# Fused attention and two MLPs on one core: the last pair of a long attention block is multiplied by v behind the next block's first tile, and v is loaded a head earlier

## The chip, the cores and the metric

One core of a Trainium2 chip runs the whole program in one launch. The metric is the device time of the execution in microseconds; lower is better. A run before the change takes 764.3 us (median of three).

## The reference

Causal attention with a decay (4 batches, 8 heads, 576 rows, head width 64), then a residual MLP behind a layer norm, then a gated MLP with a product over the sequence:

```python
scores = scale * np.matmul(q, k.transpose(0, 1, 3, 2))
decay = cum[:, :, :, None] - cum[:, :, None, :]
scores = np.where(causal, -1000000000.0, scores + decay)
...
attn = attn / (np.sum(attn, axis=-1, keepdims=True) + 1e-09)
return np.matmul(attn, v).astype(np.float32)
...
ch = np.maximum(xn @ w_ch1, 0.0) @ w_ch2
return (x + ch).astype(np.float32)
...
v_s = np.einsum('ts,bsd->btd', w_spatial, v_n) + b_spatial[None, :, None]
gated = u * v_s
return (gated @ w_out).astype(np.float32)
```

Here `cum` is the running sum of log f along the rows, `xn` the layer norm of x, `u` and `v_n` the two halves of relu(x @ w_in), the second one normed.

## The kernel before

Attention is cut into eight blocks of 256 rows of x (`BLOCKS`), and the first MLP into seven groups that follow them one group behind. Blocks 0 to 3 hold the first 128 and the second 128 rows of two batches each. Blocks 4 to 7 are the four long ones, one for each batch: query rows 256 to 575 against all keys up to them (`attention`, line 571). They run from about 200 to 460 us, between the matmuls of the first MLP (lines 849 and 864), of which each group has 384.

A long block goes over four pairs of heads. For each head, `operands` (line 325) loads q and k (qk) and four rows of decay into one of three buffers x2z, and splits q and k in two parts for an exact product. `weights` (line 345) then makes one tile of 128 query rows: scores on TensorE (line 359), mask and minimum on VectorE (363), exponential and sum on ScalarE (367), reciprocal (370), a high half on ScalarE (319) and a low half on VectorE (380, called `low`), and a transposing DMA of both halves from SyncE into PT (382). Tiles 2 and 3 belong to one head; tile 4, the last 64 rows, is made for both heads of the pair at once and has two cuts of 288 columns. When a pair's three tiles are transposed for both heads, `values` (line 578) multiplies them by v: 30 small matmuls into one bank (line 586), evicted by ScalarE (591, 592). v's columns for the pair are loaded as vr (610) and split in two halves vp by ScalarE and VectorE (`parts16`, 280 and 281). The product of a pair is called in the next pair, behind its second head's tile 3; the product of the last pair is called two steps after its tile 4 (lines 623 and 624).

The order of the work is written in two stages. `run` gives each block's and each MLP group's steps a time on a common line (`SPAN`, `BEGIN`, `steps`, line 1368) and calls them in that order; the next block begins before the one before it has ended. That order is a priority. The scheduler of the framework then places every instruction on its engine's queue by what it reckons to be ready, so a change of one priority shifts many places on every queue. Each engine, and SyncE's DMA queue, executes in its order. `after` adds an order between two instructions, here "not placed before".

Of the kernel before, what the change touches and what calls it, by code (L numbers as in the profile page):

```python
# [23 lines left out]
NP = H // 2  # L24
# [1 line left out]
TOK = 256  # L26
QW = S - 2 * P
SC = 2.0 ** 14
BUFS = dict(vr=1, vp=2, qk=3, x1=3, x2=3, PT=4, sd=3, st=6, P16=5, xt=1)
BUFS0 = dict(vr=1, qk=1, e=4, diag=2, PT=2, st=4)  # L30
BUFS1B = dict(vr=4, vp=4, qk=4, sd=4, P16=4, PT=3, st=8)
BUFS1 = dict(vr=3, vp=3, qk=3, sd=2, P16=2, PT=2, st=6)
# [9 lines left out]
BLOCKS = [(0, 0), (2, 0), (0, 1), (2, 1), (0, 2), (1, 2), (2, 2), (3, 2)]  # L42
# [6 lines left out]
RAMP, G1 = 1.5, 1.0  # L49
BEGIN = [0.0, G1, *(RAMP + 0.5 * i for i in range(6)), RAMP + 3.5]  # L50
E0, E1 = -0.1, 0.45
SPAN = [(-1.0, -0.6), (0.02, 0.45), (0.46, RAMP - 0.47), (RAMP - 0.46, RAMP - 0.14)]
for _n in range(4):
    SPAN.append((SPAN[-1][1] - (0.065 if _n else 0), SPAN[-1][1] + 2.39 / 4))
SPAN.append((SPAN[-1][1] - 0.034, SPAN[-1][1] + 0.02))
RAWAT = (-0.975, -0.974, -0.973)
CONV = (-0.6, 0.001, 0.002, 0.003, 0.004)
# [18 lines left out]
def qtile(i):  # L76
    return i * P, min(S, (i + 1) * P)
# [11 lines left out]
class Kernel:  # L89
# [235 lines left out]
    def operands(self, bh):  # L325

        nc, at = self.nc, self.at
        W, C = QW, QW + S
        qk = at.tile([P, C], F32, tag="qk", name="qk", bufs=BUFS["qk"])
        nc.sync.dma_start(out=qk, in_=self.qk[bh // H, bh % H])  # L330
        x1 = at.tile([P, C], F32R, tag="x1", name="x1", bufs=BUFS["x1"])
        if not self.x2z:
            for i in range(BUFS["x2"]):
                self.x2z.append(at.tile([P, C], F32R, name=f"x2z{i}"))
# [10 lines left out]
    def weights(self, i, heads):  # L345

        nc, at, bufs, q0 = self.nc, self.at, BUFS, 2 * P
        lo, hi = qtile(i)
        R, N, nb, qs, m0 = hi - lo, hi, i + 1, slice(lo - q0, hi - q0), 512 - lo
        M = R * len(heads)  # L350
        sd = at.tile([P, S], F32, tag="sd", name="sd", bufs=bufs["sd"])
        st = at.tile([P, 5], F32, tag="st", name="st", bufs=bufs["st"])
        cuts = [(0, N)] if N <= 512 else [(0, 288), (288, 576)]
        for n, (c0, c1) in enumerate(cuts):
            ps = self.bank("s")
            for u in reversed(range(len(heads))):

                for g, (x, y) in enumerate(heads[u][0]):
                    nc.tensor.matmul(  # L359
                        ps[: R * u + R, : c1 - c0], lhsT=x[:, lo - q0 - R * u : hi - q0], rhs=y[:, c0:c1],  # L360
                        start=g == 0, stop=g == len(heads[u][0]) - 1, skip_group_check=True)
            mask = self.mask4[:M] if n else self.mask[:M, m0 + c0 : m0 + c1]
            nc.vector.tensor_tensor_reduce(  # L363
                out=sd[:M, c0:c1], in0=ps[:M, : c1 - c0], in1=mask, scale=-0.125,
                scalar=3e38 if n == 0 else st[:M, n - 1 : n], op0=ALU.add, op1=ALU.min, accum_out=st[:M, n : n + 1])
        n = len(cuts) - 1
        nc.scalar.activation(sd[:M, :N], sd[:M, :N], AF.Exp, bias=st[:M, n : n + 1], scale=-1.0, accum_out=st[:M, 2:3])  # L367
        rs = st[:M, 3:4]
        nc.scalar.activation(rs, st[:M, 2:3], AF.Copy, bias=1e-9 / SC, scale=1.0 / SC)
        nc.vector.reciprocal(rs, rs)  # L370
        ph = at.tile([P, 5, 2, P], F16, tag="P16", name="P16", bufs=bufs["P16"])
        pieces = [(0, i), (i, nb)] if R < P else [(0, nb)]
        if R < P:
            nc.gpsimd.memset(ph[:M, i, :, R:], 0.0)
        for k0, k1 in pieces:
            w = P if k1 * P <= N else R
            src = sd[:M, k0 * P : k0 * P + (k1 - k0 - 1) * P + w].rearrange("p (t w) -> p t w", w=w)
            dh, dl = ph[:M, k0:k1, 0, :w], ph[:M, k0:k1, 1, :w]
            self.copy(DHE[i - 2], dh, src, rs)
            low = nc.vector.scalar_tensor_tensor(out=dl, in0=src, scalar=rs, in1=dh, op0=ALU.mult, op1=ALU.subtract)  # L380
        for u, (_, PT) in enumerate(heads):
            tr = nc.sync.dma_start_transpose(out=PT[:, : 2 * nb, qs], in_=ph[R * u : R * u + R, :nb].rearrange("p t h w -> p (t h w)"))
            self.in_order("tr", tr)
        return low


# [184 lines left out]
    def attention(self, b, xT, xt, middle=None):  # L571
        nc, at, bufs = self.nc, self.at, BUFS
        q0, W = 2 * P, QW
        stored = xt is None
        if stored:
            xt = at.tile([P, NP, S - 512], F32, tag="xt", name="xt", bufs=bufs["xt"])

        def values(p, vp, vsc, heads, behind=None):

            pav = self.bank("av")  # L580
            for kt in range(5):
                n0 = max(kt * P, q0) - q0
                for vi, pi in ((0, 1), (1, 0), (0, 0)):
                    for u in range(2):
                        us = slice(64 * u, 64 * u + 64)
                        ins = nc.tensor.matmul(  # L586
                            pav[us, n0:W], lhsT=vp[:, vi, kt, us], rhs=heads[u][1][:, 2 * kt + pi, n0:W],
                            start=(kt == 0 and (vi, pi) == (0, 1)), stop=(kt == 4 and (vi, pi) == (0, 0)), skip_group_check=True)
                        if behind is not None and kt == 0 and (vi, pi) == (0, 1):
                            self.after(ins, behind)  # L590
            nc.scalar.activation(xT[:, p, :], pav[:, :TOK], AF.Copy, scale=vsc)
            nc.scalar.activation(xt[:, p, :], pav[:, TOK:W], AF.Copy, scale=vsc)
            if p == 1:
                self.xs = self.mo_sum(xT)
            elif p == 2:
                nc.vector.tensor_tensor(out=self.xs, in0=self.xs, in1=xT[:, 2, :], op=ALU.add)

        late = None
        passes = self.operands(b * H)
        for p in range(NP):  # L600
            if middle and p == 2:
                middle()
            heads = []
            for u in range(2):
                heads.append((passes, at.tile([P, 10, W], F16, tag="PT", name="PT", bufs=bufs["PT"])))
                if 2 * p + u + 1 < H:
                    passes = self.operands(b * H + 2 * p + u + 1)
                if u:
                    vr = at.tile([P, 5, P], F32, tag="vr", name="vr", bufs=bufs["vr"])
                    nc.sync.dma_start(out=vr, in_=self.v[b, :, p * P : (p + 1) * P].rearrange("(t p) d -> p t d", p=P))  # L610
                yield
                for i in (2, 3):
                    done = self.weights(i, heads[u:])
                    if late and (u, i) == (1, 3):
                        yield
                        values(*late, done)
                    yield
            vp = at.tile([P, 2, 5, P], F16, tag="vp", name="vp", bufs=bufs["vp"])
            self.weights(4, heads)
            vsc = self.parts16(vr, vp[:, 0], vp[:, 1], b)  # L620
            late = p, vp, vsc, heads
            yield
        yield
        values(*late)
        yield
        if stored:
            nc.scalar.dma_start(out=self.xt_d[:, :, b, :], in_=xt)
        return self.xs
# [658 lines left out]
    def run(self):  # L1287
# [77 lines left out]
                yield  # L1365


        steps = [(NP * 2 + 1, NP * 6, NP * 8 + 1)[kind] + 3 for _, kind in BLOCKS] + [4]
        events = []
        for n in range(last + 1):  # L1370
            a0, a1 = SPAN[n]
            events += [(a0 + (a1 - a0) * (e + 0.5) / steps[n], 1, n) for e in range(steps[n])]
# [90 lines left out]
        for b in range(B):  # L1463
            x2 = self.load_x2(b + 1) if b + 1 < B else iter(())
# [69 lines left out]
```

## Time and profile before

| | |
|---|---|
| median of 3 runs | 764.3 us (762.98 to 765.41) |
| profiled execution | 763.16 us, of which the span of its instructions 761.2 us |
| TensorE busy | 739.7 us, 97%, clock 1.0 |
| VectorE, ScalarE busy | 590.9 us (78%), 528.8 us (69%) |
| long blocks, 200 to 460 us | TensorE 253.49, VectorE 218.41, ScalarE 209.00 us busy |

The page of a profile has the busy time of each engine, the span in 40 slices, the chain of work that ended last and the costliest groups of instructions. Beside it the trace answers questions: a timeline of one engine in a stretch, where the bracket behind a row tells how long the engine was idle before it and what ended that; a table of waits by what ended them; busy time by stretches; the chain in a stretch, in which a DMA's row runs from its issue to its landing.

### The profile page before, as it was taken

What the parts mean: (1) busy time and instruction counts of PE and PEld (TensorE: products, weight loads), DVE (VectorE), ACT (ScalarE), POOL (GpSimd) and SP (SyncE); (2) the same over time, 40 slices, a digit from 0 to 9 for tenths busy, and PEclk for the clock granted to TensorE, in tenths of its full rate; (3) what the DMA queues carried; (4) which work ended last, traced back from release to release, by engine and by line L of the source; (5) the groups of instructions that cost most, each with busy time, mean ns of one, the idle gap of its engine ahead of it and who ended that gap; (6) DMA issues with size and microseconds to landing.
All of it is one profiled execution on the core that took longest, in us unless ns stands there. A gap on an engine that the chain in (4) does not pass through costs nothing.

```text
span 761.2 us, 16265 instructions
## 1 busy us (share of the span) xinstructions
PE 739.7 (97%) x5912; PEld 567.9 (75%) x5912; DVE 590.9 (78%) x1569; ACT 528.8 (69%) x1320; POOL 67.4 (9%) x102
## 2 busy tenths in 40 slices
PE   8899998999999999999999999999999999999998
PEld 6788887888888877877888888644447678768686
DVE  7899799577599989989869845689456796785854
ACT  6898699576588989879857844587346764664633
POOL 6001100013102010110110100200012000000000
PEclk9999999999999999999999999999999999999999
DMA  8978694466589998988965944831025240100101
GB/s 263 295 269 274 206 266 84 89 171 105 176 167 206 198 220 183 195 189 177 201 144 116 148 84 149 213 132 56 1 22 111 70 125 1 44 21 7 57 2 62
DMA packets 164100, 104.68 MB, mean 138 GB/s; under 512 B 106147, under 2 KB 151299, under 8 KB 164021
## 3 DMA queue, kind: packets, MB, share of 16 engines
q1 hardware_dynamic: 153032, 93.06, 50.3%
q0 software_dynamic: 5376, 5.54, 5.2%
q10 hardware_dynamic: 5612, 5.06, 2.2%
q8 instruction: 46, 0.75, 0.4%
q14 instruction: 34, 0.27, 0.1%
HBM read 64.37 MB, written 15.11 MB: 104 GB/s over the span
## 4 chain that ended last, share of the span: by engine, by line
PE 63%; DVE 11%; ACT 10%; DMA 10%; issue 4%; SPq 2%; DVEq 0%; ACTq 0%
PE ph L864 16%; PE acc L849 12%; PE pb L808 8%; PE pb L809 8%; PE pb L810 8%; DMA raw<-in_moe_w_ch_dram 3%; PE s L359 3%; PE s L849 3%; DMA vr<-in_v_dram 2%; PE av L586 2%; ACT wt L744 2%; ACT P L319 2%; DMA x_d<-xT 2%; DVE P L380 1%; DMA qk<-decay 1%
## 5 line engine op out<-in xcount | busy, mean ns | idle before, releaser
L849 PE MATMUL acc<-hh,wt 128*128 128x256 f16 (+2 forms) x960 | 196.8, 295 | 3.2 <-ACT hh L875 3.2
L864 PE MATMUL ph<-xh,wt 128*128 128x256 f16 (+1 forms) x896 | 185.0, 288 | 2.0 <-DVE hl L879 2.0
L864 PEld LDWEIGHTS <-wt 128*128 128x128 f16 x1344 | 126.9, 98 | 47.4 <-issue 10.2
L849 PEld LDWEIGHTS <-wt 128*128 128x128 f16 x1344 | 128.7, 98 | 44.3 <-issue 5.3
L864 PE MATMUL ph<-xl,wt 128*128 128x256 f16 (+1 forms) x448 | 129.0, 288 | 0.0
L849 PE MATMUL acc<-hl,wt 128*128 128x256 f16 (+1 forms) x416 | 115.8, 281 | 1.1 <-DVE hl L879 1.1
L875 ACT ACTIVATE hh<-ph 128x256 f16<-128x256 f32 (+2 forms) x128 | 50.9, 397 | 45.8 <-PE ph L864 45.5
L879 DVE SCALAR_TENSOR_TENSOR hl<-ph,hh 128x256 f16<-128x256 f32 (+1 forms) x112 | 50.5, 453 | 35.9 <-ACT hh L875 35.7
L319 ACT ACTIVATE P<-sd,st 128x512 f16<-128x512 f32 (+2 forms) x128 | 70.6, 585 | 9.8 <-DVE st L370 6.9
L380 DVE SCALAR_TENSOR_TENSOR P<-sd,st,P 128x384 f16<-128x384 f32 (+2 forms) x96 | 59.2, 634 | 10.5 <-ACT P L319 10.3
L367 ACT ACTIVATE sd<-sd,st 128x384 f32<-128x384 f32 (+2 forms) x80 | 54.6, 682 | 14.4 <-DVE st L363 14.2
L359 PE MATMUL s<-x2z 128*128 128x384 f32 (+3 forms) x128 | 47.8, 382 | 1.9 <-DMA x2z<-decay_d 1.7
L363 DVE CUSTOM_DVE_ANT_0 sd<-s,mask 128x384 f32<-128x384 f32 (+2 forms) x80 | 46.0, 579 | 3.7 <-PE s L359 2.7
L900 POOL DMA_DIRECT2D x_d<-t x36 | 31.9, 1024 | 182.7 <-DVE t L896 153.1
L359 PE MATMUL s<-x 128*128 128x384 f32 (+3 forms) x128 | 41.4, 333 | 0.0
L809 PE MATMUL pb<-wsl,vh 128*128 128x288 f16 x128 | 36.6, 286 | 0.0
L808 PE MATMUL pb<-wsh,vl 128*128 128x288 f16 x128 | 36.6, 286 | 0.0
L810 PE MATMUL pb<-wsh,vh 128*128 128x288 f16 x128 | 36.4, 286 | 0.0
L810 PE MATMUL pb<-gh,woh 128*128 128x288 f16 x128 | 35.0, 286 | 0.0
L809 PE MATMUL pb<-gl,woh 128*128 128x288 f16 x128 | 35.0, 286 | 0.0
L808 PE MATMUL pb<-gh,wol 128*128 128x288 f16 x128 | 33.3, 286 | 0.0
L922 ACT ACTIVATE gh<-u 128x288 f16<-128x288 f32 x32 | 14.0, 437 | 26.5 <-DVE u L1261 26.5
(341 smaller groups left out, 1692.5 us busy)
## 6 DMA issues: line engine op xcount, KB each, us to landing
raw<-in_moe_w_ch_dram SPq DMA_DIRECT2D x32, 512.0 KB
qk<-in_qk_dram SPq DMA_DIRECT2D x32, 448.0 KB
vraw<-in_v_dram SPq DMA_DIRECT2D x5, 1024.0 KB
vr<-in_v_dram SPq DMA_DIRECT2D x16, 320.0 KB
x_d<-t POOLq DMA_DIRECT2D x36, 128.0 KB, 4.3
out_dram<-o SPq DMA_DIRECT2D x32, 144.0 KB
raw<-in_moe_w_in_dram SPq DMA_DIRECT2D x8, 512.0 KB
qk<-in_qk_dram SPq DMA_DIRECT2D x16, 192.0 KB
```

The source lines that it names most:

```text
L319: self.nc.scalar.activation(out, in_, AF.Copy, scale=scale)
L359: nc.tensor.matmul(ps[: R * u + R, : c1 - c0], lhsT=x[:, lo - q0 - R * u : hi - q0], rhs=y[:, c0:c1], start=g == 0, stop=g == len(heads[u] ...
L363: nc.vector.tensor_tensor_reduce(out=sd[:M, c0:c1], in0=ps[:M, : c1 - c0], in1=mask, scale=-0.125, scalar=3e38 if n == 0 else st[:M, n - 1 ...
L367: nc.scalar.activation(sd[:M, :N], sd[:M, :N], AF.Exp, bias=st[:M, n : n + 1], scale=-1.0, accum_out=st[:M, 2:3])
L380: low = nc.vector.scalar_tensor_tensor(out=dl, in0=src, scalar=rs, in1=dh, op0=ALU.mult, op1=ALU.subtract)
L808: first = mm(out, lhsT=al, rhs=bh, start=start, stop=False, **kw)
L809: mm(out, lhsT=ah, rhs=bl, start=False, stop=False, **kw)
L810: mm(out, lhsT=ah, rhs=bh, start=False, stop=stop, **kw)
L849: ins = nc.tensor.matmul(acc[m], lhsT=a, rhs=b, start=bank not in clear, stop=last and e == len(terms) - 1, skip_group_check=True)
L864: ins = nc.tensor.matmul(ph, lhsT=a, rhs=b, start=k == e == 0, stop=k == NK - 1 and e == len(terms) - 1)
L875: relu = nc.scalar.activation(hh, ph, AF.Relu)
L879: nc.vector.scalar_tensor_tensor(out=hl, in0=ph, scalar=0.0, in1=hh, op0=ALU.max, op1=ALU.subtract)
```

## The change

Three edits, with their consequences in the tables of steps. The buffer of vr gets a second copy, and v is loaded with a pair's first head instead of its second. The product of a block's last pair is called three steps after its tile 4 and two more (`LATER`) steps of the block exist, so that it is called when the next block has begun. And its first matmuls are placed behind `self.low`, the low half of the tile that was made last by then: one of the next block's first tiles, or in the last block its own tile 4.

```diff
-BUFS = dict(vr=1, vp=2, qk=3, x1=3, x2=3, PT=4, sd=3, st=6, P16=5, xt=1)
+BUFS = dict(vr=2, vp=2, qk=3, x1=3, x2=3, PT=4, sd=3, st=6, P16=5, xt=1)
...
+LATER = 2
 SPAN = [(-1.0, -0.6), (0.02, 0.45), (0.46, RAMP - 0.47), (RAMP - 0.46, RAMP - 0.14)]
 for _n in range(4):
-    SPAN.append((SPAN[-1][1] - (0.065 if _n else 0), SPAN[-1][1] + 2.39 / 4))
+    _a = SPAN[3][1] + 2.39 / 4 * _n - 0.065 * (_n > 0)
+    _b = SPAN[3][1] + 2.39 / 4 * (_n + 1)
+    SPAN.append((_a, _b + (_b - _a) / 28 * LATER))
...
+        self.low = low
         return low
...
-                if u:
+                if not u:
                     vr = at.tile([P, 5, P], F32, tag="vr", name="vr", bufs=bufs["vr"])
                     nc.sync.dma_start(out=vr, in_=self.v[b, :, p * P : (p + 1) * P].rearrange("(t p) d -> p t d", p=P))
...
-        yield
-        values(*late)
+        for _ in range(1 + LATER):
+            yield
+        values(*late, self.low)
...
-        steps = [(NP * 2 + 1, NP * 6, NP * 8 + 1)[kind] + 3 for _, kind in BLOCKS] + [4]
+        steps = [(NP * 2 + 1, NP * 6, NP * 8 + 1 + LATER)[kind] + 3 for _, kind in BLOCKS] + [4]
```

In the changed file line 359 stands at 362, 382 at 385, 610 at 614, 338 at 341, 586 at 590, and 849 and 864 at 854 and 869.

**TensorE, end of the first long block.** From the last scores of its last pair (bank s2_3324) to the product by v (av). Of the matmuls in between, those of the MLP (ph, acc) and of other tiles' scores are left out. Before:

```order
L359 MATMUL s2_3324<-x2z0_2347 64x288
L359 MATMUL s2_3324<-x1_2917 64x288
...
L864 MATMUL ph_4076<-xl_3606,wt_171 128x256
L586 LDWEIGHTS vp_3315
L586 MATMUL av_3372<-PT_3101,vp_3315 64x320
L864 LDWEIGHTS wt_171
L864 MATMUL ph_4076<-xh_3605,wt_171 128x256
L359 MATMUL s2_3692<-x2z1_2349 128x384
L359 MATMUL s2_3692<-x1_3534 128x384
...
L586 MATMUL av_3372<-PT_3194,vp_3315 64x320
```

And now:

```order
L362 MATMUL s2_3324<-x2z0_2347 64x288
L362 MATMUL s2_3324<-x1_2919 64x288
...
L362 MATMUL s2_3694<-x2z1_2349 128x384
L362 MATMUL s2_3694<-x1_3513 128x384
...
L869 MATMUL ph_4153<-xh_3603,wt_171 128x256
L590 LDWEIGHTS vp_3315
L590 MATMUL av_3448<-PT_3101,vp_3315 64x320
L590 LDWEIGHTS vp_3315
L590 MATMUL av_3448<-PT_3196,vp_3315 64x320
```

The first matmul of the product stood alone, ahead of a tile of the next block's second pair, with the other 29 behind; now all 30 stand together behind that tile. Between the last scores and the first of the 30 there were 64 matmuls of the MLP and are 99.

**TensorE, last pair of the last long block.** From the last scores of the pair before (s2_6509, the last reader of x2z1) to the last head's first scores (s2_6643, which read x2z1 as newly loaded). Before:

```order
L359 MATMUL s2_6509<-x2z1_2349 64x288
L359 MATMUL s2_6509<-x1_6053 64x288
...
L359 MATMUL s2_6556<-x2z0_2347 128x384
L359 MATMUL s2_6556<-x1_6334 128x384
...
L359 MATMUL s2_6643<-x2z1_2349 128x384
```

And now:

```order
L362 MATMUL s2_6509<-x2z1_2349 64x288
L362 MATMUL s2_6509<-x1_6055 64x288
...
L362 MATMUL s2_6558<-x2z0_2347 128x384
L362 MATMUL s2_6558<-x1_6336 128x384
...
L362 MATMUL s2_6643<-x2z1_2349 128x384
```

The rows are the same, but in between there were 36 matmuls of the MLP and the 30 of a product by v, and now there are 14 matmuls of the MLP and no product.

**SyncE, the same place.** The queue's transposing DMAs (PT), loads of v (vr) and of decay rows (x2z). Before:

```order
L382 DMA_TRANSPOSE PT_6238<-P16_6298 128x8x128
L610 DMA vr_6610<-in_v_dram 128x5x128
L382 DMA_TRANSPOSE PT_6331<-P16_6380 128x6x128
L338 DMA x2z1_2349<-decay_d_68 4x896
L382 DMA_TRANSPOSE PT_6331<-P16_6393 128x8x128
```

And now:

```order
L385 DMA_TRANSPOSE PT_6238<-P16_6329 128x8x128
L385 DMA_TRANSPOSE PT_6333<-P16_6380 128x6x128
L385 DMA_TRANSPOSE PT_6333<-P16_6393 128x8x128
L341 DMA x2z1_2349<-decay_d_68 4x896
L385 DMA_TRANSPOSE PT_6238<-P16_6518 128x10x64
```

The load of v has left this place (it went out with the pair's first head), and the load of x2z1 stands behind both of the second head's first two transpositions instead of one.

## Rows read from the trace of the kernel before

**Rows 1.** The page, part 1: busy us, share of the span and instructions.

```profile
PE 739.7 (97%) x5912; PEld 567.9 (75%) x5912; DVE 590.9 (78%) x1569; ACT 528.8 (69%) x1320; POOL 67.4 (9%) x102
```

**Rows 2.** Busy time by stretches: length, then each engine, granted clock, DMA.

```profile
200.00:460.00 260.00, 253.49 (x2342) 210.30 (x2340) 218.41 (x593) 209.00 (x542) 26.04 (x40) 1.00 0.85 167
```

**Rows 3.** TensorE's waits from 190 to 470 us: total, times, longest.

```profile
PE av L586 <- DMA PT<-P: 2.7, 2, 1.7
PE s L359 <- DMA x2z<-decay_d: 1.7, 2, 1.5
PE acc L849 <- DVE hl L879: 1.1, 1, 1.1
```

**Rows 4.** The chain from 425 to 435.5 us: start, us, what.

```profile
427.48 1.06 PE s L359 x8
...
429.32 1.68 PE av L586 x30
...
431.66 0.81 PE s L359 x4
...
433.79 1.31 PE acc L849 x12
```

**Rows 5.** TensorE's timeline (start, us, instruction), end of the first long block.

```profile
254.77 0.29 PE L359 MATMUL s<-x 128*64 128x288 f32 x1
...
266.45 0.27 PE L864 MATMUL ph<-xl,wt 128*128 128x256 f16 x1
268.40 0.30 PE L586 MATMUL av<-PT,vp 128*64 128x320 f16 x1 [1.68 <-DMA PT<-P]
```

**Rows 6.** The same, end of the second long block.

```profile
310.05 0.28 PE L849 MATMUL acc<-hl,wt 128*128 128x256 f16 x1
...
324.55 0.30 PE L586 MATMUL av<-PT,vp 128*64 128x320 f16 x1 [1.04 <-DMA PT<-P]
```

**Rows 7.** The same, third long block, third pair.

```profile
339.70 0.28 PE L849 MATMUL acc<-hh,wt 128*128 128x256 f16 x1
...
348.41 0.41 PE L359 MATMUL s<-x2z 128*128 128x384 f32 x1 [1.49 <-DMA x2z<-decay_d]
```

**Rows 8.** The same, fourth long block, first pair's second head.

```profile
378.76 0.41 PE L359 MATMUL s<-x2z 128*128 128x384 f32 x1 [0.26 <-DMA x2z<-decay_d]
```

**Rows 9.** Fourth long block, last pair: timelines of three engines, and the chain's end.

```profile
428.39 0.28 PE L864 MATMUL ph<-xh,wt 128*128 128x256 f16 x1
...
428.38 2.66 POOL L900 DMA_DIRECT2D x_d<-t  x3 [2.27 <-DVE t L896]
...
430.33 0.70 SPq L338 DMA_DIRECT2D x2z<-decay_d  x1
...
435.10 0.12 issue
435.22 0.41 PE s L359
```

**Rows 10.** The chain behind v's load, first long block; then TensorE's timeline.

```profile
208.88 3.36 DMA vr<-in_v_dram
...
218.93 0.27 PE L864 MATMUL ph<-xh,wt 128*128 128x256 f16 x1 [0.71 <-DVE hl L879]
```

**Rows 11.** TensorE's timeline, end of the third long block.

```profile
372.23 0.39 PE L849 MATMUL acc<-hh,wt 128*128 128x256 f16 x2
...
385.21 0.32 PE L586 MATMUL av<-PT,vp 128*64 128x320 f16 x1
...
386.56 0.73 PE L586 MATMUL av<-PT,vp 128*64 128x320 f16 x8
```

**Rows 12.** The chain over the whole span: two loads of x2z, issue to landing.

```profile
346.27 2.01 DMA x2z<-decay_d
...
373.04 5.58 DMA x2z<-decay_d
```

**Rows 13.** Busy time by stretches, as in the second group.

```profile
340.00:360.00 20.00, 18.51 (x169) 15.52 (x169) 19.49 (x53) 18.64 (x50) 0.66 (x3) 1.00 0.83 166
```

## Prediction, made before the changed kernel was run

> **What bounds the kernel now.** The page's first part says TensorE is busy for 739.7 of 761.2 us, 97% [rows 1]: only time in which TensorE stands still can be won. The table of stretches says where that is in the part that the change touches: from 200 to 460 us, while attention and the first MLP share the engines, TensorE is busy 253.49 of 260 us at a granted clock of 1.00, and VectorE 218.41 and ScalarE 209.00 [rows 2]. So there are 6.5 us to win there and no more. The table of waits names what ended TensorE's idle time [rows 3]: the transposed weights PT (a DMA) before the product by v, 2.7 us in two waits; the decay rows loaded into x2z before a tile's scores, 1.7 us; hl from VectorE, 1.1 us, beside a shorter one.
>
> The timeline then gives the place of each. An MLP matmul is shown 0.27 us wide, but the next one starts 0.11 us later (12 take 1.31 us [rows 4]), so a wait costs 0.16 us more than the idle time printed: at 268.40 the loss is 268.40 - 266.45 - 0.11 = 1.84 us where 1.68 is printed [rows 5]. With that the waits cost: product by v at the end of the first long block 1.84 and of the second 1.20 [rows 5, 6]; scores behind x2z 1.65, 0.42 and 0.28 [rows 7, 8, 9]; hl 0.87 and 1.27 [rows 3, 10].
>
> **How much cover each of them has.** Between the end of a pair's last scores and its product by v, TensorE does other work; the transposed weights need a fixed chain in that time (mask, exponential, sum, two halves, transposing DMA). In the first long block the last scores end at 254.77 + 0.14 = 254.9 and the weights are there at 268.40: the chain needs 13.5 us [rows 5]. In the second it is 324.55 - 310.05 = 14.5 [rows 6]. In the third no wait is shown: at most 385.21 - 372.23 = 13.0 for the first head's weights and 386.56 - 372.23 = 14.3 for the second's [rows 11].
>
> The order before puts 64, 79 and 86 MLP matmuls between the two in these blocks, plus other blocks' scores and one earlier product by v. At 0.109 us a matmul, 1.68 for a product by v, 0.81 for a head's first two tiles and 1.06 for a tile of both heads [rows 4] that is 11.5, 13.2 and 12.4 us of cover. The order of the changed kernel has 99, 111 and 96 matmuls, and one more pass of scores in the first two: 15.8, 17.1 and 13.3 us. In the fourth block it has 77 both before and after: there the operand named as "behind" is the block's own last tile, so nothing moves.
>
> **The change part by part.**
> The move of the last product: 15.8 us of cover against 13.5 needed, and 17.1 against 14.5. Both waits go: -1.84 - 1.20 = -3.04 us. What they give back isn't lost to a later stage: xT of a long block is used by the MLP group that begins some 270 MLP matmuls later (about 30 us), so the norm, its SyncE and ScalarE stores and the split of x can all come 4 us later at no cost; that cover would have to shrink by tens of us to matter. In the third block the product now is in one piece of 30, so it needs both heads' weights, between 13.0 and 14.3 us after the scores, and has 13.3. A wait of 0 to 1.0 us; I take 0.4, a little under the middle, as nothing shows that the second head's weights came only just before they were read.
>
> v's load: it moves from the pair's second head to its first, into the other buffer. 16 loads before and after, and as many conversions; nothing is added. What goes is that SyncE's queue must hold the load until VectorE has converted the pair before. That shows at the start of the first long block: v's load leaves at 208.88, right behind that conversion, and lands 3.36 us later, ScalarE goes on with it at once, and the chain ends in the hl for which TensorE waits at 218.93 [rows 10]. In the new order both conversions stand early, but the same exponentials and both heads' conversions of q and k still stand ahead of that hl. Of 0.87 us between all and nothing is won; I take half, -0.4.
>
> What the two parts shift in SyncE's and TensorE's orders: each second head's x2z has to wait for the last scores of the pair before (the buffer is shared), then passes SyncE's queue and lands. In the third block's third pair this needs 348.41 - 339.70 = 8.7 us [rows 7]; TensorE's order had 6.8 us of work in that time and now has 79 matmuls and two tiles, 9.8 us: -1.65. At the fourth block's first pair it needs 6.5 us [rows 11, 8] and now has over 13: -0.42. At the last pair of the last block it is the other way: the order before has 36 matmuls, a product by v and two tiles, 6.5 us, and the need is 435.22 - 428.39 = 6.8 [rows 9]; the new order has 14 matmuls and two tiles, 1.53 + 0.81 = 2.3 us. Here the price of the load decides. It lands 2.01 us after its issue where the queue is quiet, 5.58 where other transfers are under way, and at this place 435.10 - 430.33 = 4.8 [rows 12, 9]; before it, SyncE spent 1.9 us after the release on v's load and a transposition, which now stand earlier. With 0.4 us to issue, the need lies between 2.4 and 6.8 us, so the new wait between 0 and 4.5. The nearest row is this load's own, since the accumulating stores of the MLP group that ends here, three of them from 428.38 on [rows 9], stay at this place: 0.4 + 4.8 = 5.2, a wait of 2.9, which with the 0.28 of before is +2.6.
>
> The Trainium skill has a rule for this price: the page "DMA: Bandwidth & Descriptors", section "Anatomy of one DMA", gives a fixed cost of about 2.0 us and a part that grows with the size (told there of GpSimd's queue). By it the 14 KB would land in 2.0 us and the new wait would be nothing, the sum -5.4; the 2.01 us row agrees, the 4.8 and 5.58 rows do not.
>
> The second hl wait (1.27) and what the scheduler reshuffles on VectorE and ScalarE I leave at nothing: same instructions, same counts, other order.
>
> Sum: -3.04 + 0.4 - 0.4 - 1.65 - 0.42 + 2.6 = -2.5 us. The profiled execution took 763.16 us, so 760.7 against it; that execution lies 1.1 under the median of 764.3, and against the median the forecast is **761.8 us**. A measurement of this kernel can tell about 0.3%, 2.3 us, from no change: faster is below 762.0, slower above 766.6.
>
> **The rivals.**
> Quiet load: the last x2z lands in 2 us, as at 346.27 [rows 12]. No new wait: -2.5 - 2.9 = -5.4, 758.9 us. For it: v's load, which stood directly before it, is gone from there. Against it: the stores at the group's end stay. This is also what the page's rule above gives. Chance 0.22.
>
> The waits only change their place: the last x2z needs the full 6.8 us although v's load is gone (wait 4.5 instead of 2.9), the third block's product pays its full 1.0, and the early hl gives back nothing. -2.5 + 1.6 + 0.6 + 0.4 = +0.1: 764.4 us, no change. For it: two of three x2z waits on record landed late [rows 9, 12]. Chance 0.20.
>
> Slower, by VectorE: the chain from scores to transposed weights gets longer by d, since the next block's first tiles now are handled in the same stretch, and VectorE is busy 19.49 of 20 us from 340 to 360 [rows 13]. Then everything behind SyncE's transpositions comes later by d: the third block's product and the last x2z each lose d from the first bit, the third block's third pair from d = 1.1, the two products that were won from d = 2.3 and 2.6. For d = 2 that is 2 + 2 + 0.9 = +4.9 over the forecast, the point from which it is slower; for d = 3 it is 3 + 3 + 1.9 + 0.7 + 0.4 = +9.0, 770.8 us. Against it: in SyncE's order the last pair's transpositions stay ahead of the next block's, and the three last pairs on record need 13.5, 14.5 and 13.0 to 14.3 us, close to each other. Chance 0.13.
>
> **How the numbers follow.** The forecast itself has 0.45, and as it lies at the edge of what can be told, 0.25 of it falls on faster and 0.20 on no change. Faster 0.25 + 0.22 = 0.47, same 0.20 + 0.20 = 0.40, slower 0.13. The range runs from 758.7, just under the quiet load, to 766.2: it leaves out the slower case and what of the quiet load goes further, some 2 in 10.
>
> **What would show it.** In the changed profile the waits for PT before the product by v should be gone from the ends of the first two long blocks, with at most 1 us in the third; x2z should end one wait of 2 to 4 us before the last pair of the last block and none in the third block; no ScalarE wait for v's load. TensorE's idle time from 200 to 460 should fall from 6.5 to about 4 us. Wrong would be: a wait for PT of over 1 us, hl waits of over 3 us in sum, or idle time as large as before.

## The result and the profile after

The changed kernel takes 770.5 us (median of 8 runs, 767.95 to 772.86) where the kernel before, run beside it, takes 765.4 (8 runs, 762.98 to 768.9): ratio 1.0071, 95% interval 1.0047 to 1.0094. It is slower by 0.7%; forecast were 761.8 us, and a range up to 766.2. The profiled execution is the slowest of the eight, 772.86 us with a span of 770.9, 9.7 more than before's.

The page's first part, then the table of stretches, of the changed kernel (columns as in [rows 1, 2]):

```profile
PE 743.5 (96%) x5912; PEld 570.5 (74%) x5912; DVE 592.0 (77%) x1569; ACT 529.2 (69%) x1320; POOL 67.9 (9%) x102
```

```profile
200.00:460.00 260.00, 247.83 (x2256) 205.32 (x2255) 217.41 (x589) 208.14 (x538) 26.56 (x40) 0.99 0.86 171
```

The counts are those of [rows 1]: no work was added. TensorE's idle time from 200 to 460 us went from 6.5 us [rows 2] to 260 - 247.83 = 12.2; 4 was forecast. TensorE's waits from 190 to 480 us say what ended it (total, times, longest):

```profile
PE av L590 <- DMA PT<-P: 3.1, 2, 2.7
PE ph L869 <- DVE hl L884: 2.6, 2, 1.7
PE s L362 <- DVE st L366: 2.2, 3, 1.1
PE s L362 <- ACT P L322: 1.5, 1, 1.5
PE s L362 <- DVE x2z L345: 1.1, 1, 1.1
PE s L362 <- DMA x2z<-decay_d: 0.6, 1, 0.6
```

Against [rows 3], loads of x2z fell from 1.7 to 0.6 by this table (the 1.5 us put down to ACT are a load of x2z too, as shown below), but VectorE (hl, the masked scores' st, its own half of x2z) now ends 6 us of waits. TensorE's timeline shows the places:

```profile
221.04 0.27 PE L869 MATMUL ph<-xh,wt 128*128 128x256 f16 x1 [0.89 <-DVE hl L884]
...
250.02 0.41 PE L362 MATMUL s<-x2z 128*128 128x384 f32 x1 [1.48 <-ACT P L322]
...
272.76 0.73 PE L590 MATMUL av<-PT,vp 128*64 128x320 f16 x8
...
283.53 0.27 PE L869 MATMUL ph<-xh,wt 128*128 128x256 f16 x1 [1.74 <-DVE hl L884]
...
304.45 0.47 PE L362 MATMUL s<-x2z 128*128 128x512 f32 x1 [1.06 <-DVE st L366]
...
307.87 0.41 PE L362 MATMUL s<-x2z 128*128 128x384 f32 x1 [1.13 <-DVE x2z L345]
...
310.48 0.50 PE L362 MATMUL s<-x2z 128*128 128x512 f32 x1 [0.93 <-DVE st L366]
...
335.23 0.32 PE L590 MATMUL av<-PT,vp 128*64 128x320 f16 x1
...
394.19 0.30 PE L590 MATMUL av<-PT,vp 128*64 128x320 f16 x1 [2.73 <-DMA PT<-P]
...
441.52 0.41 PE L362 MATMUL s<-x2z 128*128 128x384 f32 x1 [0.63 <-DMA x2z<-decay_d]
```

At 272.76 and 335.23 the products that waited in [rows 5, 6] start without a wait, as forecast. At 394.19 the third block's product waits. The hl wait at 221, which was to shrink, is as long as before. At 250, 283 and in a group from 303 to 311 there are waits that nobody forecast.

From here on a **standstill** is worked out from the trace thus: the time from one matmul's start to the next one's, less the median of that time for matmuls of the same line and shape, counted where it is over 0.25 us and placed at the first of the two. From 190 to 480 us before has 7 of them, 7.6 us together; the change has 15, 14.8 us. These 7.2 us are most of the 9.7 us. A further 1.4 us or so are in a slow stretch behind the group; the table of stretches shows it (the granted clock is the third number from the end). The last 1.1 us are not placed.

```profile
300.90:310.90 10.00, 6.52 (x46) 4.37 (x43) 9.27 (x25) 8.87 (x21) 3.71 (x5) 1.00 0.98 178
310.90:314.30 3.40, 3.40 (x31) 2.20 (x30) 2.86 (x9) 1.41 (x5) 0.00 (x0) 0.50 1.18 232
314.30:317.70 3.40, 3.40 (x37) 2.99 (x34) 1.84 (x3) 3.16 (x9) 0.00 (x0) 1.00 1.25 161
```

TensorE was busy for 6.52 of 10 us, then ran for 3.4 us at the lower of its two levels (0.50, 1.2 GHz). This isn't the main cause: the three of the eight runs with a mean granted clock of 0.999 or 1.000 took 768.0, 769.1 and 770.9 us.

### The profile page after: what moved, and what is told of

It is laid out like the page before. It is cut to its first block, busy times and chain, and to the rows that moved or that the text cites. A ratio compares the mean times of both kernels' runs of the same rounds, so it can differ in the third digit from the quotient of the medians.

```text
span 770.9 us, 16275 instructions
## 1 busy us (share of the span) xinstructions
PE 743.5 (96%) x5912; PEld 570.5 (74%) x5912; DVE 592.0 (77%) x1569; ACT 529.2 (69%) x1320; POOL 67.9 (9%) x102
## 4 chain that ended last, share of the span: by engine, by line
PE 62%; DVE 14%; ACT 10%; DMA 8%; issue 5%; SPq 1%; DVEq 0%; ACTq 0%
PE ph L869 14%; PE acc L854 12%; PE pb L813 8%; PE pb L815 8%; PE pb L814 8%; PE s L362 3%; DMA x_d<-xT 2%; PE av L590 2%; DVE P L383 2%; ACT wt L749 2%; ACT P L322 2%; DVE sd L366 2%; PE s L854 1%; DMA raw<-in_moe_w_in_dram 1%; DVE x2z L345 1%
## 5 line engine op out<-in xcount | busy, mean ns | idle before, releaser
L383 DVE SCALAR_TENSOR_TENSOR P<-sd,st,P 128x384 f16<-128x384 f32 (+2 forms) x96 | 58.4, 630 | 10.4 <-ACT P L322 10.1
L370 ACT ACTIVATE sd<-sd,st 128x512 f32<-128x512 f32 (+2 forms) x80 | 54.8, 685 | 13.1 <-DVE st L366 12.6
L590 PE MATMUL av<-PT,vp 128*64 128x320 f16 (+2 forms) x480 | 30.4, 278 | 3.1 <-DMA PT<-P 3.1
```

## The experiments

My theories to begin with: **Late product** (the moved product lengthens the chains behind it), **Early loads** (v's load, moved ahead, does the harm), **Reshuffle** (any edit makes the scheduler write an order that is worse by chance). Later texts call the last one "order", and split the second into "two buffers" and "early load". All runs are compared with the kernel before on the same chip (median 762.9 to 765.0 us in the five groups). Standstills from 190 to 480 us and in two places, in us:

| kernel | ratio to before (95%) | all | 244-250 | 298-312 |
|---|---|---|---|---|
| before | 1 | 7.6 | 0.0 | 1.3 |
| the change | 1.0071 (1.0047-1.0094) | 14.8 | 1.6 | 4.6 |
| v_only | 1.0048 (1.0029-1.0068) | 13.2 | 1.5 | 4.3 |
| late_only | 1.0069 (1.0044-1.0094) | 13.8 | 0.0 | 2.1 |
| shift_minus | 0.9992 (0.9971-1.0012) | 7.4 | 0.0 | 1.6 |
| norm_low | 1.0090 (1.0059-1.0121) | 13.1 | 0.8 | 4.2 |
| two_buffers | 1.0074 (1.0049-1.0099) | 14.5 | 2.6 | 4.3 |
| early_one | 1.0069 (1.0045-1.0093) | 13.0 | 0.0 | 0.3 |
| late_early_one | 1.0029 (1.0006-1.0052) | 8.7 | 0.0 | 0.3 |
| later_1 | 1.0070 (1.0046-1.0094) | 13.5 | 1.9 | 4.3 |
| vp_three | 1.0033 (1.0013-1.0054) | 11.1 | 2.9 | 2.6 |
| span_wide | 0.9966 (0.9948-0.9984) | 7.7 | 0.0 | 1.3 |
| shift_plus | 0.9997 (0.9973-1.0020) | 8.9 | 0.0 | 2.0 |
| late_early_shift | 1.0038 (1.0012-1.0064) | 14.2 | 0.0 | 0.3 |
| change_wide | 1.0026 (1.0001-1.0052) | 11.2 | 1.8 | 4.1 |
| v_wide | 1.0033 (1.0010-1.0055) | 11.7 | 1.8 | 4.1 |
| late_wide | 0.9976 (0.9956-0.9995) | 6.4 | 0.0 | 1.8 |
| late_early_wide | 1.0030 (1.0007-1.0053) | 10.1 | 0.0 | 0.3 |
| v_shift | 1.0062 (1.0043-1.0081) | 12.3 | 2.4 | 4.1 |
| late_shift | 0.9991 (0.9970-1.0013) | 7.0 | 0.0 | 2.1 |

### Each part alone

v_only is the kernel before with

```
-BUFS = dict(vr=1, ...
+BUFS = dict(vr=2, ...
-                if u:
+                if not u:
```

> The kernel before with the two edits on v alone: two buffers for vr, and the load with the pair's first head. Three theories. Late product: the later product by v is the cause, because it moves the finished block's norm and split into a stretch where VectorE and ScalarE are full; then this kernel is within 1 us of the one before, without the idle stretch of about 6 us that TensorE has from 303 to 311 us in the changed kernel. Early loads: v's load a head earlier crowds the queue, so the transposed weights of the third long block's last pair land late (7.8 us after their issue instead of 3.6); then this kernel is slower by 3 to 5 us and shows that wait of 3.5 us. Reshuffle: any shift of a priority deals the scheduler's order anew, and the loss belongs to neither part; then it may lie anywhere within 5 us of the one before.

late_only is the change without these two edits.

> The changed kernel with one buffer for vr and v's load back with the pair's second head: the later product alone. Late product: slower than before by 4 to 6 us, as the changed kernel. Early loads: the two waits for PT at the ends of the first two long blocks are gone and nothing else, so 1 to 3 us faster than before. Reshuffle: anywhere within 5 us of before, with its idle time at other places than in the changed kernel.

shift_minus moves only the long blocks' start in the scheduler's table:

```
-    SPAN.append((SPAN[-1][1] - (0.065 if _n else 0), ...
+    SPAN.append((SPAN[-1][1] - (0.060 if _n else 0), ...
```

> The kernel before, with the one number that says how much a long block overlaps the one before it changed from 0.065 to 0.060, about a quarter of a step: no part of the change is in it. Late product and early loads: within 1 us of before. Reshuffle: 2 us or more away from before, to either side.

Each part alone costs nearly as much as both (767.5 and 769.9 us against 763.8), so the two do not add up; the small reshuffle costs nothing. No theory foresaw this whole: v_only's time is that of "Early loads", but the wait at the third block's end that was to come with it is not there. v_only has the change's own places, in TensorE's timeline:

```profile
248.23 0.41 PE L359 MATMUL s<-x2z 128*128 128x384 f32 x1 [1.37 <-DMA x2z<-decay_d]
...
300.40 0.42 PE L359 MATMUL s<-x2z 128*128 128x384 f32 x1
...
303.08 0.47 PE L359 MATMUL s<-x2z 128*128 128x512 f32 x1 [1.08 <-DVE st L363]
...
306.51 0.41 PE L359 MATMUL s<-x2z 128*128 128x384 f32 x1 [1.13 <-DVE x2z L342]
...
307.80 0.38 PE L849 MATMUL acc<-hh,wt 128*128 128x256 f16 x2 [0.26 <-ACT hh L875]
...
309.11 0.50 PE L359 MATMUL s<-x2z 128*128 128x512 f32 x1 [0.94 <-DVE st L363]
```

What is ahead of the scores at 303.08 on VectorE, by its timeline in v_only:

```profile
300.90 0.87 DVE L896 TENSOR_SCALAR t<-acc,und 128x256 f32<-128x256 f32 x2
301.68 0.88 DVE L281 SCALAR_TENSOR_TENSOR vp<-vr,vsc,vp 128x640 f16<-128x640 f32 x1
302.47 0.45 DVE L363 CUSTOM_DVE_ANT_0 sd<-s,mask 128x288 f32<-128x288 f32 x1
```

Two of an MLP group's evictions and v's conversion go before the mask whose st (302.85) lets the scores go on. Before, that conversion is at 295.17 and the first eviction at 302.73, with the split of x (L828) between 296.3 and 298.5; in v_only the split runs from 299.1 to 306.6, among both heads' conversions of q and k. The instructions are the same, but conversion, evictions and split now fall together.

TensorE's own order changed as well. The scores of the pair's two heads, two tiles each, start at 300.40, 303.08, 306.51 and 309.11 in v_only; before, the first and the last of them are

```profile
296.33 0.42 PE L359 MATMUL s<-x2z 128*128 128x384 f32 x1
...
304.24 0.48 PE L359 MATMUL s<-x2z 128*128 128x512 f32 x1
```

The tiles took 8.7 us in v_only, of which VectorE was busy 8.6, and 7.9 before, of which it was busy 7.8. Between them stand 9, 12 and 6 matmuls of the MLP in v_only, as in the change, and 12, 11 and 24 before. These 20 fewer matmuls, at 0.109 us, are 2.2 of the 3.1 us that the group grew by in v_only (1.27 to 4.33); the slower tiles are the other 0.8. The stretch, before and in v_only:

```profile
298.00:312.00 14.00, 12.85 (x121) 10.26 (x119) 12.73 (x36) 12.25 (x34) 3.52 (x4) 1.00 1.08 201
```

```profile
298.00:312.00 14.00, 10.49 (x94) 7.56 (x93) 13.27 (x37) 11.74 (x29) 3.71 (x5) 1.00 0.96 184
```

VectorE is busy 13.27 of 14 us instead of 12.73, TensorE 10.49 instead of 12.85.

Behind the wait at 248 (250 in the change) is a load of x2z. In the change the table puts it down to ACT's P, which ends at the same moment, but in v_only and v_shift the same scores start before that instruction has ended. SyncE's timeline before, then in the change:

```profile
239.74 0.95 SPq L610 DMA_DIRECT2D vr<-in_v_dram  x1
240.79 0.43 SPq L338 DMA_DIRECT2D x2z<-decay_d  x1
241.31 1.22 SPq L382 DMA_TRANSPOSE PT<-P  x1
242.62 0.43 SPq L338 DMA_DIRECT2D x2z<-decay_d  x1
```

```profile
242.47 0.70 SPq L614 DMA_DIRECT2D vr<-in_v_dram  x1
243.27 1.56 SPq L385 DMA_TRANSPOSE PT<-P  x1
244.93 0.79 SPq L341 DMA_DIRECT2D x2z<-decay_d  x2
```

A transposition has come between v's load and the first x2z load: it starts 2.5 us behind v's instead of 1.05, the two land at 249.5 and 249.9, and the scores start at 250.02. But the queue is only a part of it. A buffer of x2z is free when the last scores of the pair before have read it. The last of these scores, and before also the next scores that need the load, are these rows, before and in the change:

```profile
240.42 0.30 PE L359 MATMUL s<-x 128*64 128x288 f32 x1
...
248.77 0.42 PE L359 MATMUL s<-x2z 128*128 128x384 f32 x1
```

```profile
243.45 0.29 PE L362 MATMUL s<-x 128*64 128x288 f32 x1
```

In the change the first of the two loads leaves 1.3 us behind the end of these scores (0.2 before), and the later one has landed 6.3 us behind it. TensorE's order before has 68 matmuls of the MLP and two tiles up to the scores at 248.77, 8.2 us of cover; the change has 36 and two tiles up to those at 250.02, 4.7 us. By this count the order of before would have covered even the late load. All eight kernels with the second buffer have the 36.

The wait at 283 is another matter. VectorE's timeline, before and in the change:

```profile
277.91 1.41 DVE L782 TENSOR_TENSOR xT<-xT,av 128x256 f32<-128x256 f32 x4 [0.28 <-DMA x_d<-xT]
```

```profile
281.73 1.41 DVE L787 TENSOR_TENSOR xT<-xT,av 128x256 f32<-128x256 f32 x4 [2.52 <-DMA x_d<-xT]
283.06 0.41 DVE L884 SCALAR_TENSOR_TENSOR hl<-ph,hh 128x256 f16<-128x256 f32 x1
```

Here VectorE isn't full: it stands idle for 2.5 us, since the norm may overwrite xT only when its store has landed, and the hl that TensorE needs stands behind. The store took 6.2 us instead of 4.4. In the eight kernels with the second buffer two loads of q and k (448 KB each) are issued beside it, the second from 0.3 us ahead of it to 0.15 behind, and it takes 6.2 to 7.1 us; in the other twelve the second is 2.0 to 3.0 us ahead and it takes 4.3 to 5.9. That the loads hold it up is likely by this, not tried.

late_only's loss is in another place. TensorE's timeline, ScalarE's, and the chain of waits from 425 to 440 us:

```profile
436.81 0.59 PE L854 MATMUL acc<-hh,wt 128*128 128x256 f16 x2 [4.71 <-ACT hh L880]
```

```profile
435.66 0.83 ACT L283 ACTIVATE vp<-vr,vsc 128x640 f16<-128x640 f32 x1 [6.66 <-DMA vr<-in_v_dram]
436.39 0.36 ACT L880 ACTIVATE hh<-ph 128x256 f16<-128x256 f32 x1
```

```profile
429.68 5.96 DMA vr<-in_v_dram
435.63 0.02 issue
435.66 0.83 ACT vp L283
```

v's load, with the second head and into one buffer, left 2 us later than before (427.69) and took 6 us; v's conversion stood ahead of hh in ScalarE's queue, and TensorE stood still for 4.9 us. Behind that the clock again was granted at 0.50, for 6.8 us:

```profile
435.40:442.20 6.80, 4.84 (x21) 3.04 (x21) 4.48 (x14) 6.01 (x17) 0.00 (x0) 0.50 0.07 13
```

norm_low is the change with the long blocks' norm at ordinary priority:

```
-                    with self.tc.high_priority(1):
+                    with nullcontext() if 4 <= n < last else self.tc.high_priority(1):
```

> The changed kernel, with the norm of the long blocks at ordinary priority instead of ahead of everything else; TensorE's order is the same as in the changed kernel, only VectorE's, ScalarE's and the DMA queues' differ. Late product: the norm no longer stands before the tiles' rows, so TensorE's idle stretch from 303 to 311 us shrinks by half or more and the kernel is 2 to 4 us faster than the changed one. Early loads: as the changed kernel, 5 us slower than before. Reshuffle: no direction follows.

The group stayed (4.2 us), so the norm's priority isn't its cause. TensorE has the change's order here (9, 12 and 6 matmuls between the tiles), and the tiles took only 8.0 us, as before:

```profile
301.96 0.42 PE L362 MATMUL s<-x2z 128*128 128x384 f32 x1
...
309.93 0.79 PE L362 MATMUL s<-x2z 128*128 128x512 f32 x1 [0.93 <-DVE st L366]
```

Still TensorE stood still for 3.6 us between them, where before has 1.3. So the larger part of the group goes with TensorE's order. No run has that order of TensorE with the VectorE order of before, so how the group divides between the two rests on the count.

### Which half of v's move, and whether the late product needs it

two_buffers has vr=2 alone, early_one "if not u" alone; late_early_one is the change with vr=1, later_1 the change with LATER = 1.

> The kernel before with two buffers for v, its load still issued with a pair's second head; TensorE's order of instructions is then that of v_only, and only a few loads and conversions stand elsewhere. Theory 'two buffers': what cost v_only its 3.7 us is the order that the scheduler makes once a second buffer is there (both conversions, the norm's split and the group's evictions in one stretch at 293 to 309 us), so this run is as slow: 767.5 us, within 1, with the standstills at 301 to 309 us (about 4.3 us together). Theory 'early load': it is the load's earlier transfer that delays others; then this run is 764 us and has no standstills there. Theory 'noise of the order': neither, anything from 761 to 768, and standstills in other places.

> The kernel before with v's load issued with a pair's first head, but into one buffer. Theory 'two buffers': without the second buffer the stretch at 293 to 309 us stays as it was before, and the load comes early where the buffer is free, so ScalarE's two waits for v (0.9 and 1.3 us) shrink: 763 to 764 us. Theory 'early load': as slow as v_only, 767.5 us. Theory 'noise of the order': anything from 761 to 768.

> The whole change with one buffer for v instead of two. In late_only 4.9 us of its loss stood in one place: at 431.7 us ScalarE had v's conversion ahead of the MLP's hh in its queue, v's load was issued at 429.7 and landed at 435.6, and TensorE stood still until hh came; a stretch at the granted clock of 0.5 followed. Theory 'v behind the late product': the load issued with the first head takes that wait away, the second buffer is not needed for it, and what is left is the gain at the blocks' ends: 762 to 765 us, no TensorE standstill over 2 us that ends on hh. Theory 'two buffers': the same, since the stretch at 301 to 309 us comes back only with the second buffer. Theory 'the late product itself costs': 769 to 771 us, with PT waits at the third block's end and chains 2 to 4 us longer.

> The whole change with the last pair's product one step later instead of two. The burst at 301 to 309 us comes from v's buffers and should stay (about 4 us). Theory 'v costs, the lateness gains': about 768 to 771 us, as the change, with a part of the PT waits at the blocks' ends back. Theory 'the late product itself costs' in proportion to how late it is: half way between v_only and the change, 769 us. Theory 'noise of the order': anything from 763 to 772, with standstills in places that neither parent has.

two_buffers has v_only's places over again though its loads are issued with the second head: the group from 298 to 312 us belongs to the second buffer and the order that comes with it. But early_one, without the group, is as slow. It has standstills of its own (x2z at 258.11, 1.9 us, and at 320.57, 2.8 us; the third block's product at 389.54, 3.3 us), so "two buffers" is not the whole of it either. late_early_one has no TensorE standstill behind v (ScalarE waits for it twice, 1.5 us at most) and 8.7 us of standstills in all, yet it isn't faster than before: "v behind the late product" missed by 0.3%, as its interval excludes 1. later_1 has v_only's places and the change's time (1.0070).

### Orders alone

vp_three has vp=3 in BUFS; shift_plus 0.070 in place of 0.065; span_wide

```
-    SPAN.append((SPAN[-1][1] - (0.065 if _n else 0), SPAN[-1][1] + 2.39 / 4))
+    SPAN.append((SPAN[-1][1] - (0.055 if _n else 0), SPAN[-1][1] + 2.42 / 4))
```

late_early_shift is late_early_one with 0.060.

> The kernel before with three buffers in place of two for v's converted halves: nothing on the chip has to wait longer for that, no transfer or product is moved on purpose, but the scheduler writes another order, in which 1132 rows of TensorE's list differ (1092 in the change). Theory 'order': a new order of that size by itself exposes other waits of one to three us between 190 and 400 us: 765 to 769 us. Theory 'the change's own terms' (v's load, the late product): 763 us, within 1.5. Theory 'two buffers' in its narrow form (the second raw buffer alone): 763 as well.

> The kernel before with the long blocks' stretches 0.03/4 longer and starting 0.055 instead of 0.065 ahead: 754 rows of TensorE's list differ, no part of the change is in it. Theory 'order': 764 to 768 us, with standstills of one to three us where before has none. Theory 'the change's own terms': 763 us, within 1.5.

> The kernel before with the stretches starting 0.070 instead of 0.065 ahead, the other side of shift_minus: 236 rows of TensorE's list differ (384 in shift_minus). Theory 'order': between no difference and 2 us, 763 to 765, since few rows move. Theory 'the change's own terms': 763 us, within 1.

> late_early_one with the stretches starting 0.060 instead of 0.065 ahead: its lateness, its one buffer and its early load stay, 616 rows of TensorE's list differ from it. Theory 'order': late_early_one was one good order among several, so this one lies anywhere from 762 to 770 us. Theory 'the change's own terms', by which the late product with an early load into one buffer is the good version and the second buffer the bad part: 765 us or less, no burst at 301 to 309 us.

A reshuffle is worth anything from -0.34% to +0.33% by itself. So a single comparison of two kernels can't tell a part's own cost from its order's, and span_wide, which holds nothing of the change, beats both kernels.

### The same parts on two other bases

change_wide, v_wide, late_wide and late_early_wide are the change, v_only, late_only and late_early_one with span_wide's 0.055 and 2.42; v_shift and late_shift are v_only and late_only with shift_minus' 0.060.

> The whole change on the base of span_wide (761.9 us). Theory 'the change's own terms': it loses there what it loses on the kernel before, 0.7%: 767 us, with the standstills at about 301 to 309 us and no PT wait at the first two long blocks' ends. Theory 'order': any loss from 0 to 1%, 762 to 769 us, with standstills in other places than in the change.

> v's second buffer and earlier load alone, on the base of span_wide. Theory 'the change's own terms': 0.5% over that base, 765.7 us, with four or five standstills of 0.3 to 1.3 us at 300 to 310 us. Theory 'order': 761 to 768 us, and no such group there.

> The late product alone, on the base of span_wide; one buffer, v loaded with the second head. Theory 'the change's own terms': as late_only against before, 0.6% over its base, 766.5 us, with a standstill of some 5 us behind v's conversion in the last long block. Theory 'order': 759.5 to 768 us; where v's load happens to land before its conversion's turn there is no such standstill, and the 2.5 us of PT waits at the first two long blocks' ends are gained: 759.5 to 761.5 us.

> The late product with v's load at the first head into one buffer, on the base of span_wide. Theory 'the change's own terms' (this is the good version of the change): 0.3% over its base, 764 us or less. Theory 'order': anything from 760 to 769 us (1318 rows of TensorE's list differ from the base).

> v's second buffer and earlier load alone, on the base of shift_minus (763.0 us). Theory 'v costs by its own terms': 0.4 to 0.8% over that base, 766 to 769 us, with the waits for x2z at about 246 us (1.5 to 2.4 us) and the group at 301 to 309 us (3 to 5 us) that all seven kernels with the second buffer showed. Theory 'order': 761 to 768 us without one or both of these.

> The late product alone on the base of shift_minus. Theory 'neutral unless v lands late': 761.5 to 764.5 us, PT waits of 1 to 3 us left at the first long block's end (TensorE's list has as little work ahead of that product as before), no standstill over 3 us. Theory 'the late product costs by itself': 768 us, as late_only.

Against its own base, v's part costs 0.48% on the kernel before, 1.0033 / 0.9966 = 0.67% on span_wide and 1.0062 / 0.9992 = 0.70% on shift_minus (each quotient good to about 0.3%), and shows the same places each time; v_shift's timeline:

```profile
248.73 0.48 PE L359 MATMUL s<-x2z 128*128 128x384 f32 x1 [1.96 <-DMA x2z<-decay_d]
...
305.15 0.47 PE L359 MATMUL s<-x2z 128*128 128x512 f32 x1 [1.08 <-DVE st L363]
...
310.97 0.37 PE L864 MATMUL ph<-xh,wt 128*128 128x256 f16 x1 [1.57 <-DVE hl L879]
```

All eight kernels with the second buffer have 4.1 to 4.6 us of standstills from 298 to 312 and 0.8 to 2.6 at 244 to 250. The four with the early load into one buffer are all but free of both, but slower by 0.3 to 0.7% with x2z or its scores late at 320.

The late product alone costs 0.69%, 0.10% and -0.01% against its bases: nothing that can be told, except where v's load lands behind its conversion's turn (late_only). It gains nothing either, since the first block's product still waits in late_shift:

```profile
267.37 0.30 PE L590 MATMUL av<-PT,vp 128*64 128x320 f16 x1 [1.57 <-DMA PT<-P]
```

## Why the prediction was wrong, point by point

**What bounds the kernel**: right. TensorE's standstills decide it, and they are what moved.

**The last product's waits, -3.04 us**: the two waits went, so the term came, but the step gave it to the wrong part. v_only, which doesn't move the product, has 0.47 us left of the first wait and none of the second; the late product alone keeps 1.4 us (late_only), 2.5 (late_wide) or 1.7 (late_shift) of the first. Costed as in the prediction, TensorE's order has 11.5 us of work ahead of the first block's product before, 15.7 in the change, 14.1 in v_only, 12.7 in late_only and 11.5 in late_wide and late_shift: a place two steps later in the table need not be later among TensorE's instructions.

**Third block, +0.4**: it cost 2.89 + 0.57 = 3.5 us. From the last scores to the transposition's issue it took as long as before (386.23 - 377.89 = 8.3 us; 8.65 before), but the two transpositions landed 7.8 and 6.1 us after their issue, where I had 3.6 and 3.7 in the need of 13.0 to 14.3. Two loads of q and k left just ahead of them at 382.94 and 383.58 and landed at about 391. That these held the transpositions up is argued, not shown. No other kernel with the late product waits that long there, and early_one, without it, waits 3.3 us for the same product, so that wait needs no late product.

**v's load, -0.4**: ScalarE's waits for v are gone, as I said. The hl wait at the first block's start is not smaller (1.05 us beside 0.52 for the scores before it; 0.87 before), and the load's new place, which I costed at nothing else, pushed x2z's loads behind a transposition.

**x2z in the third and fourth block, -1.65 and -0.42**: right, both gone. **The last x2z, +2.6**: 0.8 instead of 0.28, so +0.5; the cover was the 2.3 us of the sum, and the load landed in 3.0 us, between the quiet 2.0 and the 4.8 I took. The Trainium skill's rule for it (page "DMA: Bandwidth & Descriptors", section "Anatomy of one DMA", told there of GpSimd's queue: a fixed cost of about 2.0 us and a part by size) gives an estimate of 2 us. The trace does not agree: 3.0 here, and 4.6 for the load issued at 244.93 in the change.

**"What the scheduler reshuffles on VectorE and ScalarE I leave at nothing: same instructions, same counts, other order"**: this is the step that failed, and TensorE's and SyncE's orders belong to it. The prediction counted cover only where before showed a wait or where the product moved. The new waits are at places where before has none or a short one: 3.3 us more in the group at 303 to 311 (4.6 where 1.27 stood), where TensorE has 27 matmuls of the MLP between a pair's tiles instead of 47 and VectorE, all but full, sets the pace of the tiles; 1.6 at 250, where TensorE's cover for a load of x2z fell from 8.2 to 4.7 us; and 1.9 at 283, where hl stood in VectorE's queue behind a store that took longer. That is 6.8 us, with the 1.4 us of slow clock behind them. All three places are also in the kernels with v's part alone. The norm's store, which the step on the product let off as able to come 4 us later at no cost, is the one at 283; v_only, whose product is not late, has that wait too (1.5).

Summed over standstills: -3.06 + 3.46 + 0.70 (hl and the scores before it at 219 to 221) - 1.65 - 0.42 + 0.52 + 6.8, and 0.84 for two short new ones, is +7.2 us, where -2.5 was forecast.

**The rivals**: "slower, by VectorE" had the direction and the engine, but the price came another way. The chains from scores to transposed weights cost nothing in the first two blocks; VectorE held up the next scores and hl themselves. That its 770.8 us for d = 3 lies beside the 770.5 measured is luck.

Open: why a second buffer makes the scheduler put conversion, evictions and split together and take matmuls of the MLP out from between the scores; and whether v loaded early but converted in its old place would be free of it. The second wasn't tried.

## What to carry to other kernels

An edit "with the same instructions" changes the list order of all engines, and the order may cost more than the wait it was to remove. So count the cover in the new order at every place where TensorE depends on a load or on a nearly full engine, not only where the profile of before shows a wait: two of the three new costs here could have been read as lost matmuls in TensorE's order before the run. Test a part on two or three neutral shifts of the schedule before believing a difference under 0.7%: here neutral edits alone spanned 0.7%, and only the repeat told v's steady cost from the late product's accident.

## What was not expected of the hardware

Short standstills of TensorE can be followed by stretches at a granted clock of 0.50 (1.2 GHz), here of 3.4 us behind the group in the change (310.9) and of 6.8 behind 4.9 us in late_only (435.4). They don't follow every standstill: the 2.73 us wait before 394.19 in the change left the clock at 1.00. And transfers of one kind vary more than their sizes say: transposing DMAs of the changed kernel landed 2.7 to 9.4 us after their issue.
